# A dilated convolution with gates on one core: warm-up on zeros, a tail with early row transposes and split stores, and a new order for the scheduler

## The chip, the core and the metric

The kernel runs on one core of a Trainium2 chip. The metric is the device time of one execution in microseconds (us), lower is better. The engines of the core are TensorE (PE, with its weight loads as PEld), VectorE (DVE), ScalarE (ACT), GpSimd (POOL) and SyncE (SP), which here only issues DMAs.

## The reference

```python
B, T, D, K = (2, 16000, 144, 15)      # x: (B, T, D), w: (K, D, 2D), w_o: (D, D), all bf16
pad = (K - 1) * 2                      # dilation 2
xp = jnp.pad(x, ((0, 0), (pad, 0), (0, 0)))
h = jnp.einsum('btc,cd->btd', xp[:, pad:pad + T, :], w[0])
for i in range(1, K):
    off = pad - i * 2
    h = h + jnp.einsum('btc,cd->btd', xp[:, off:off + T, :], w[i])
f = h[..., :D]
g = h[..., D:]
return (jnp.tanh(f) * jax.nn.sigmoid(g)) @ w_o
```

A causal convolution over time with 15 taps, two steps apart, takes 144 channels to 288; the halves go through tanh and sigmoid, are multiplied, and a 144 x 144 matrix makes the output.

## The kernel before

**Tiling.** The 32,000 time steps lie as 128 partitions by 250 steps: each partition holds one stretch of time. The steps of all partitions are worked through in "octs" of eight steps, 31 in all. One matmul has 128 of the channels of one step (for 128 partitions) as stationary tile and 288 weight columns as moving data, so its output is one step of 128 stretches. The 16 channels left over are gathered eight steps at a time into tiles of 128 (XB), whose matmuls use the weights WB.

**Fewer matmuls by differences.** Taps and steps are combined as in a fast FIR filter: DVE forms differences of input tiles (V, DU, DD, BD between octs, `ef`, `diff`, `vdiff`, L731; GX, GU, GV, GD between pairs of octs, L805 to L817) and, once at the start, sums of weights (WC, WS, WD, WT, WV, L666). The products are put together again in PSUM: ACT copies partial sums from bank to bank (`copy`, L967) or into SBUF (UC, UD, XS, through `evict`, L475 and L478), POOL adds two of these into UX (L1004), DVE makes UE (written as Xp in the profile, L994) and adds UE and UX to the banks (L1068). Nearly all matmuls are issued from L823.

**Units.** Octs 1 to 30 go in 15 pairs, each pair in two units (even and odd steps), 30 units in all; oct 0 and the end of the oct ahead of it are computed more directly in a prologue. A unit u consists of blocks of matmuls, and the next unit's blocks stand between them: for unit u EF (on GV, L823; the DVE adds L1068 follow it) and DD (on GD and BD, with the weights WA and WB), for unit u + 1 CV, CD, XC, XR, SR and UP, which prepare the common sums. PJ is one third of an oct's projection. A gate on ACT and DVE (`halves`, L475/L478; `gate`, L848) makes Z; a DMA transposes Z into ZT (`ship`, L908); `project` multiplies ZT by w_o (L925), ACT casts into OS (L929), and a DMA stores an oct (L935).

**Loads.** x comes in chunks Xr of 16 steps (L517). ACT or DVE copies it compactly into STA (L691, L694), a DMA transposes STA into XA (L696). For the 16 channels left over DVE copies them into C (L682), a DMA transposes C into T (L718), and DMAs on SP bring T by way of DRAM (s) and the previous XB into XB (all at L708). All those DMAs, the transposes of Z and the stores share SP's queue and run in its order.

**What sets the order.** The code adds operations to a graph, with their dependences and a guessed duration. `schedule` and `run` simulate the engines with these guesses and fix the order of each engine's instructions before anything is built. PE takes ready operations in program order, looking at most PE_WIN operations ahead; the other engines take the one that is due first. A load that is chained by `first` gets a guessed end. ORDER holds two strings, for even and odd units, that give the program order of the blocks above. Banks of PSUM are handed out in the same simulation. So durations in the code move instructions, but have no other effect.

**Start and tail.** While the first loads are under way, PE runs 28 matmuls that nobody reads, with the identity ID and the tile ONES, both made by POOL (`warm`, L590); then it transposes the first steps of x (L618), which ACT and DVE evict into XA (L624), and DVE writes zeros into the padding (L632). The last unit's four gates don't go to Z but into rows ZL (in the profile Xr). `project_some` (L947) projects the even steps of octs 29 and 30 from ZT; `ship_pair` transposes the rows of ZL on PE (L880), copies them (L871) and projects them (L885), and `cast` (L871) brings the result to OS. The two octs are stored at L899, each in one DMA. After its last store SP waits for the semaphores of all DMAs in turn; then the program ends.

## Time and profile before

| what | value |
|---|---|
| three runs | 309.06, 309.23, 310.7 us, median 309.23 us |
| profiled execution, its own time | 308.58 us |
| its span, from first to last instruction | 306.85 us (the page rounds it to 306.9) |
| PE, DVE, ACT, POOL busy | 98%, 94%, 84%, 33% of the span |
| mean granted TensorE clock | 0.999 |
| DMA | 48.48 MB, 158 GB/s on average |

The profile describes one execution, the profiled one. Its page gives busy time, the chain of work that ended last, and the costliest groups of instructions; the views of the trace give single instructions with start and duration, and behind an arrow what ended the idle time ahead of them. A row with a count (x28) covers consecutive instructions of one kind from the start of the first to the end of the last. L823 is line 823 of the kernel before. In the kernel after the change the lines of the same operations are 4 to 11 higher: L666 becomes L670, L682 L686, L731 L735, L823 L827, L994 L1003, L1068 L1077, L925 L933, L947 L956, L885 L893, L880 L883.

### The profile page before, as it was taken

To read this page: it belongs to the slowest core of one execution; us is meant where nothing else is said; L and a number is where in the kernel's file an instruction comes from. 1 tells how busy PE (TensorE), PEld (TensorE's weight loads), DVE (VectorE), ACT (ScalarE), POOL (GpSimd) and SP (SyncE) were. 2 spreads that over 40 slices of the span, in tenths; PEclk is the share of its full clock that TensorE was granted. 3 is DMA by queue.
4 is the path that set the end of the run, shared out by engine and by line. 5 is a ranking of instruction groups with operands and counts; after the bars stand their busy time and mean duration, and the time that the engine had idled before them with its cause. 6 is when DMAs were issued, how large, how long until landed. Compare 5 with 4: busy or idle time off the path is not lost.

```text
span 306.9 us, 7442 instructions
## 1 busy us (share of the span) xinstructions
PE 299.9 (98%) x2547; PEld 235.7 (77%) x2547; DVE 289.7 (94%) x652; ACT 257.2 (84%) x812; POOL 99.8 (33%) x89
## 2 busy tenths in 40 slices
PE   7999999999999999999999999999999999999995
PEld 6777676778787787788787787777778777877784
DVE  2899999999999999999999999999999999999764
ACT  4476788988888998888898888899888889988884
POOL 7560342223333213333311333321233332123330
PEclk9999999999999999999999999999999999999999
DMA  7976647567596774759555595866647772562342
GB/s 203 310 135 152 149 138 171 118 185 179 168 169 210 121 195 127 179 168 191 180 129 139 175 179 173 159 189 146 184 134 183 191 168 62 139 132 64 93 119 115
DMA packets 100241, 48.48 MB, mean 158 GB/s; under 512 B 88269, under 2 KB 90893, under 8 KB 100203
## 3 DMA queue, kind: packets, MB, share of 16 engines
q1 hardware_dynamic: 99657, 47.62, 62.9%
q0 software_dynamic: 512, 0.33, 0.5%
q8 instruction: 20, 0.33, 0.5%
q14 instruction: 18, 0.15, 0.2%
q10 hardware_dynamic: 34, 0.05, 0.1%
HBM read 13.77 MB, written 10.20 MB: 78 GB/s over the span
## 4 chain that ended last, share of the span: by engine, by line
PE 90%; ACT 3%; DMA 2%; SPq 2%; DVE 2%; issue 1%
PE PS L823 80%; PE PS L925 9%; ACT TG L475 1%; DMA WA<-in_w_dram 1%; SPq L517 1%; DMA XB<-XB 1%; ACT PS L967 1%; DVE OS L871 1%; SPq L696 0%; SPq L528 0%; DVE Xr L871 0%; DVE WC L666 0%; ACT TG L478 0%; PE PS L654 0%; ACT UD L478 0%
## 5 line engine op out<-in xcount | busy, mean ns | idle before, releaser
L1004 POOL TENSOR_TENSOR UX<-UC,XS 128x576 f32<-128x576 f32 x60 | 84.0, 1421 | 192.8 <-ACT UC L475 134.7
L823 PE MATMUL PS<-WA,GD 128*128 128x288 bf16 x450 | 87.4, 286 | 0.0
L967 ACT ACTIVATE PS<-PS 128x288 f32<-128x288 f32 x213 | 81.3, 437 | 0.4 <-PE PS L823 0.2
L823 PE MATMUL PS<-WB,BD 128*128 128x288 bf16 x240 | 67.5, 286 | 0.0
L475 ACT ACTIVATE TG<-PS 128x288 bf16<-128x288 f32 x140 | 51.0, 432 | 14.4 <-PE PS L823 14.3
L929 ACT ACTIVATE OS<-PS 128x432 bf16<-128x432 f32 (+1 forms) x88 | 42.5, 503 | 14.7 <-PE PS L925 14.5
L823 PEld LDWEIGHTS PS<-WA,GD 128*128 128x128 bf16 x450 | 42.5, 98 | 12.9 <-DVE PS L1068 1.5
L478 ACT ACTIVATE TG<-PS 128x144 bf16<-128x144 f32 x220 | 46.0, 310 | 6.1 <-PE PS L823 6.1
L1068 DVE TENSOR_TENSOR PS<-PS,Xp 128x288 f32<-128x288 f32 x120 | 49.5, 457 | 0.9 <-PE PS L823 0.4
L1068 DVE TENSOR_TENSOR PS<-PS,UX 128x288 f32<-128x288 f32 x120 | 49.2, 455 | 0.1
L994 DVE TENSOR_TENSOR Xp<-PS,UD 128x576 f32<-128x576 f32 x60 | 43.2, 750 | 3.1 <-ACT UD L475 1.6
L823 PE MATMUL PS<-WS,GU 128*128 128x288 bf16 x210 | 44.8, 286 | 0.3 <-DMA XB<-XB 0.2
L925 PE MATMUL PS<-WOR,ZT 128*128 128x144 bf16 (+1 forms) x322 | 40.7, 253 | 0.0
L823 PE MATMUL PS<-WB,XB 128*128 128x288 bf16 x140 | 37.6, 286 | 0.0
L823 PE MATMUL PS<-WC,GV 128*128 128x288 bf16 x210 | 35.8, 287 | 0.4 <-ACT PS L967 0.4
L925 PEld LDWEIGHTS PS<-WOR,ZT 128*128 128x128 bf16 x322 | 27.8, 98 | 5.4
L823 PE MATMUL PS<-WD,DD 128*128 128x288 bf16 x210 | 31.2, 286 | 0.0
L848 DVE TENSOR_TENSOR Z<-TG 128x576 bf16<-128x576 bf16 (+1 forms) x63 | 27.5, 438 | 2.4 <-ACT TG L475 2.0
L823 PEld LDWEIGHTS PS<-WB,BD 128*128 128x128 bf16 x240 | 23.5, 98 | 5.9
L823 PEld LDWEIGHTS PS<-WS,GU 128*128 128x128 bf16 x210 | 19.8, 98 | 6.3 <-ACT PS L967 1.4
L823 PEld LDWEIGHTS PS<-WD,DD 128*128 128x128 bf16 x210 | 19.8, 98 | 6.2 <-ACT PS L967 0.9
L823 PE MATMUL PS<-WT,DU 128*128 128x288 bf16 x120 | 24.5, 286 | 0.0
(93 smaller groups left out, 469.2 us busy)
## 6 DMA issues: line engine op xcount, KB each, us to landing
out_dram<-OS SPq DMA_DIRECT2D x31, 288.0 KB, 2.5
Xr<-in_x_dram SPq DMA_DIRECT2D x15, 576.0 KB, 4.5
XB<-XB SPq DMA_DIRECT2D x30, 192.0 KB, 3.2
XB<-s SPq DMA_DIRECT2D x59, 32.0 KB, 1.9
s<-T SPq DMA_DIRECT2D x30, 32.0 KB, 3.4
WA<-in_w_dram SPq DMA_DIRECT2D x2, 288.0 KB, 4.2
ZT<-Z SPq DMA_TRANSPOSE x32, 3.1
Xp<-in_x_dram SPq DMA_DIRECT2D x2, 252.0 KB, 4.0
```

What stands on the lines that cost most here:

```text
L475: return e.activation(bass.AP(t[:].tensor, off + (0 if st > 0 else n), [[row, NP], [st, 2], [1, n]]), bass.AP(PS[:].tensor, lo * 512 + c0, ...
L478: ins = e.activation(bass.AP(t[:].tensor, off + i * n, [[row, NP], [1, n]]), bass.AP(PS[:].tensor, q.phys * 512 + c0, [[8 * 512, NP], [1, ...
L517: return e.dma_start(tile_ap, src)
L823: return lambda t: t.matmul(bank(b), lhsT=lhs(), rhs=rhs(), start=start, stop=True, skip_group_check=True)
L848: g.add("dve", lambda v: v.tensor_tensor(dst(), TG[:, s, 1, 2 * k:2 * k + n, :], TG[:, s, 0, 2 * k:2 * k + n, :], ALU.mult), r=[("TG", s, ...
L871: return (lambda e: e.activation(dst(), src(), ACT.Copy)) if eng == "act" else (lambda e: e.tensor_copy(dst(), src()))
L925: return t.matmul(PS[:, c0:c0 + n * D], lhsT=ZT[:, zt, blk_, :], rhs=WOR[:, wi_:wi_ + n, :].rearrange("p a b -> p (a b)"), start=first, st ...
L929: g.add("act", lambda e: e.activation(OS[:, os_, a:c, :].rearrange("p e d -> p (e d)"), PS[:, bo.phys * 512:bo.phys * 512 + (c - a) * D], ...
L967: g.add("act", lambda e: e.activation(bank(c), bank(b), ACT.Copy), r=[("bank", b)], w=[("bank", c)], dur=0.29, prio=prio)
L994: return v.tensor_tensor(ue(u % NU, q, 0, 2).rearrange("p (v n) -> p v n", v=2), src, UD[:, u % NUD, :, :], ALU.add)
L1004: op = g.add("pool", lambda p: p.tensor_tensor(UX[:, u % NU, h, :, :], UC[:, 0, :, :], bass.AP(XS[:].tensor, h * N2, [[2 * N2, NP], [0, 2] ...
L1068: g.add("dve", lambda e, dst=dst, src=src, ua=ua: e.tensor_tensor(bank(dst), bank(src), ua(), ALU.add), r=[("bank", src), ("UX", us, h) if ...
```

## The change

Five edits go together.

1. PE_WIN goes from 50 to 42, and both strings of ORDER are rewritten.
2. The guessed end of the loads chained by `first` comes 0.8 us earlier (`quick`); this acts on the order only.
3. The warm-up multiplies a tile HEAT of zeros by itself, which DVE clears as its first instruction, and has 34 matmuls instead of 28.
4. In the tail each gate of the last unit is followed at once by `ship_rows`: three PE transposes and a DVE copy of the rows, now in program order and not "floating" (floating operations are taken only when nothing else is ready). `ship_pair` keeps only the matmuls and the cast. `project_some` is cut two and two steps instead of three and one. Casts of oct 29 go to ACT, those of oct 30's rows to DVE, and the last third of oct 28's projection is cast on DVE instead of ACT.
5. Oct 30 is stored in two DMAs of four steps (144 KB) each instead of one of eight (288 KB).

```diff
-PE_WIN = 50
-ORDER = ("EF0 PJ EF1 XC1 CV CD0 XC0 CD1 XR0 DD00 SR0 XR1 PJ DD11 UP0 DD01 PJ UP1 SR1 DD10", "EF0 PJ EF1 DD00 XC1 CV CD0 DD01 CD1 XC0 DD10 XR1 UP0 SR0 DD11 PJ XR0 UP1 SR1 PJ")
+PE_WIN = 42
+ORDER = ("EF0 PJ EF1 XC1 CV CD0 DD00 DD01 DD10 CD1 XR1 XC0 DD11 UP0 XR0 SR0 PJ PJ SR1 UP1", "EF0 PJ EF1 XC1 CV CD0 CD1 XC0 DD00 SR0 XR0 SR1 XR1 UP0 UP1 DD01 DD10 DD11 PJ PJ")
...
-                op.end = dma_free + DMA_LAT
+                op.end = dma_free + DMA_LAT - op.quick
...
+        g.add("dve", lambda v: v.memset(HEAT[:], 0.0), w=["HEAT"], dur=0.1)
...
+            op.quick = 0.8
...
-            g.add("pe", [lambda t: t.matmul(PS[:, BANK_O * 512:BANK_O * 512 + 128], lhsT=ID[:], rhs=ONES[:], start=True, stop=True)] * n,
-                  r=["ID", "ONES"], w=[("bank", HB[BANK_O])], dur=0.07 * n)
-
-        warm(26)
+            g.add("pe", [lambda t: t.matmul(PS[:, BANK_O * 512:BANK_O * 512 + 128], lhsT=HEAT[:], rhs=HEAT[:], start=True, stop=True)] * n,
+                  r=["HEAT"], w=[("bank", HB[BANK_O])], dur=0.07 * n)
+
+        warm(32)
...
-        def ship_pair(o, h, dl, eng):
+        def ship_rows(h, dl):
+
+            q = 2 * h + (dl == 3)
+            pa = _Bank()
             c0 = h * 672 + (dl - 3) // 2 * D
             g.add("pe", [lambda t, i=i: t.transpose(PSb[:, pa.phys * 1024 + 128 * i:pa.phys * 1024 + 128 * i + 128], ZL[:, c0 + 128 * i:c0 + 128 * i + 128], ID[:]) for i in range(3)],
-                  r=[("ZL", h, 3), ("ZL", h, 7), "ID"] if dl == 3 else [("ZL", h, 7), "ID"], w=[("bank", pa)], dur=0.2, floating=True)
-            old = set(g.readers[("Xr", 0)])
-            a = g.add(eng, cast(eng, lambda: ZTL[:, q, 0:384], lambda: PSb[:, pa.phys * 1024:pa.phys * 1024 + 384]), r=[("bank", pa)], w=[("ZTL", q)], dur=0.4)
-            a.deps |= old
+                  r=[("ZL", h, 3), ("ZL", h, 7), "ID"] if dl == 3 else [("ZL", h, 7), "ID"], w=[("bank", pa)], dur=0.2)
+            a = g.add("dve", lambda e: e.tensor_copy(ZTL[:, q, 0:384], PSb[:, pa.phys * 1024:pa.phys * 1024 + 384]), r=[("bank", pa)], w=[("ZTL", q)], dur=0.27)
+            a.deps |= set(g.readers[("Xr", 0)])
...
-            g.add("act", lambda e: e.activation(OS[:, os_, a:c, :].rearrange("p e d -> p (e d)"), PS[:, bo.phys * 512:bo.phys * 512 + (c - a) * D], ACT.Copy),
+            eng = "dve" if (o, gi) == (2 * NPAIR - 2, 2) else "act"
+            g.add(eng, cast(eng, lambda: OS[:, os_, a:c, :].rearrange("p e d -> p (e d)"), lambda: PS[:, bo.phys * 512:bo.phys * 512 + (c - a) * D]),
...
-            for h, part in enumerate((dls[:3], dls[3:])):
+            for h, part in enumerate((dls[:2], dls[2:])):
...
+            ship_rows(h, 7 if k == 0 else 3)
...
-        project_some(o0, (0, 2, 4, 6), "dve")
-        ship_pair(o0, 0, 7, "dve")
-        ship_pair(o0, 0, 3, "dve")
-        store_some(o0, [0, 3, 7], 1, 8, 0)
+        project_some(o0, (0, 2, 4, 6), "act")
+        ship_pair(o0, 0, 7, "act")
+        ship_pair(o0, 0, 3, "act")
+        store_some(o0, [3, 7], 1, 8, 0)
+        ship_pair(o1, 1, 7, "dve")
+        ship_pair(o1, 1, 3, "dve")
         project_some(o1, (0, 2, 4, 6), "act")
-        ship_pair(o1, 1, 7, "act")
-        ship_pair(o1, 1, 3, "dve")
-        store_some(o1, [0, 3, 7], 1, 8, 0)
+        store_some(o1, [7], 1, 4, 4)
+        store_some(o1, [3], 1, 4, 0)
```

What the edits do to the order is read from the instructions of each engine. The first place is DVE at about 14 us of the profile, in the prologue: C is the compact copy of the 16 channels, WD and WT are sums of weights, and d_xr0 is the semaphore of the first chunk of x. Before:

```order
L731 TENSOR_TENSOR DU<-XA 128x512
L682 COPY C<-Xr 128x256 [waits d_xr0]
L731 TENSOR_TENSOR DU<-XA 128x512
L731 TENSOR_TENSOR DD<-V 128x1024 x2
L666 TENSOR_TENSOR WD<-WA 128x576 x2
L682 COPY C<-Xr 128x256 [waits d_xr1]
L666 TENSOR_TENSOR WT<-WS 128x2x288 [waits s_dve]
```

and after:

```order
L735 TENSOR_TENSOR DU<-XA 128x512 x2
L735 TENSOR_TENSOR DD<-V 128x1024
L686 COPY C<-Xr 128x256 [waits d_xr0]
L735 TENSOR_TENSOR DD<-V 128x1024
L670 TENSOR_TENSOR WD<-WA 128x576 x2
L670 TENSOR_TENSOR WT<-WS 128x2x288 [waits s_dve]
L686 COPY C<-Xr 128x256 [waits d_xr1]
```

The first copy into C has moved behind one more DU and one DD, the second behind a WT.

The second place is at about 32 us, at the end of the prologue. On PE the groups on WS,GU and WB,XB belong to XR of the first unit, those on WC,GV to its EF; d_xb9, d_xb0 and d_xb1 are semaphores of loads of XB. Before:

```order
L823 MATMUL PS<-WS,GU 128x288 [waits d_xb9,d_xb0,d_xb1]
L823 MATMUL PS<-WS,GU 128x288
L823 MATMUL PS<-WB,XB 128x288
L823 MATMUL PS<-WS,GU 128x288 x2
L823 MATMUL PS<-WB,XB 128x288
L823 MATMUL PS<-WC,GV 128x288 [waits s_dve,s_act]
L823 MATMUL PS<-WC,GV 128x288 x2
L823 MATMUL PS<-WA,GV 128x288
```

and after:

```order
L827 MATMUL PS<-WC,GV 128x288 [waits s_dve,s_act]
L827 MATMUL PS<-WC,GV 128x288 x2
L827 MATMUL PS<-WA,GV 128x288
L827 MATMUL PS<-WS,GU 128x288 [waits d_xb9,d_xb0,d_xb1]
L827 MATMUL PS<-WS,GU 128x288
L827 MATMUL PS<-WB,XB 128x288
L827 MATMUL PS<-WS,GU 128x288 x2
L827 MATMUL PS<-WB,XB 128x288
```

The group of four on GV has moved ahead of the group that waits for XB. On DVE at the same place stand the UE (Xp) sums and the adds to the banks. Before:

```order
L731 TENSOR_TENSOR V<-XA 128x1024
L994 TENSOR_TENSOR Xp<-PS,UD 128x576 [waits s_pe]
L731 TENSOR_TENSOR BD<-XB 128x1024 [waits d_xb9,d_xb0,d_xb1]
L994 TENSOR_TENSOR Xp<-PS,UD 128x576 [waits s_pe,s_dve]
L1068 TENSOR_TENSOR PS<-PS,Xp 128x288 [waits s_pe,s_act]
L1068 TENSOR_TENSOR PS<-PS,Xp 128x288 [waits s_pe]
L1068 TENSOR_TENSOR PS<-PS,Xp 128x288 [waits s_dve,s_pe]
L1068 TENSOR_TENSOR PS<-PS,Xp 128x288 [waits s_act,s_pe]
L1068 TENSOR_TENSOR PS<-PS,UX 128x288 [waits s_dve,s_pool]
L1068 TENSOR_TENSOR PS<-PS,UX 128x288 [waits s_dve]
L731 TENSOR_TENSOR DD<-V 128x1024
```

and after:

```order
L1003 TENSOR_TENSOR Xp<-PS,UD 128x576 [waits s_pe]
L735 TENSOR_TENSOR BD<-XB 128x1024 [waits d_xb9,d_xb0,d_xb1]
L1077 TENSOR_TENSOR PS<-PS,Xp 128x288 [waits s_pe,s_dve]
L1003 TENSOR_TENSOR Xp<-PS,UD 128x576 [waits s_pe]
L735 TENSOR_TENSOR V<-XA 128x1024
L1077 TENSOR_TENSOR PS<-PS,Xp 128x288 [waits s_dve]
L1077 TENSOR_TENSOR PS<-PS,Xp 128x288 [waits s_pe,s_act]
L1077 TENSOR_TENSOR PS<-PS,Xp 128x288 [waits s_act]
L735 TENSOR_TENSOR DD<-V 128x1024 [waits s_dve]
L1077 TENSOR_TENSOR PS<-PS,UX 128x288 [waits s_pool]
L1077 TENSOR_TENSOR PS<-PS,UX 128x288 [waits s_dve]
```

V has moved from ahead of the UE sums to between the adds, and DD ahead of the adds of UX.

The third place is PE's end. L925 and L947 (after: L933 and L956) project from ZT, L880 (L883) transposes the rows, L885 (L893) projects them. Before, from the last matmul of the convolution on:

```order
L823 MATMUL PS<-WB,BD 128x288
L925 MATMUL PS<-WOR,ZT 128x144 [waits s_act]
L925 MATMUL PS<-WOR,ZT 128x288
L925 MATMUL PS<-WOR,ZT 128x144
L947 MATMUL PS<-WOR,ZT 128x144 [waits d_zt0]
L947 MATMUL PS<-WOR,ZT 128x144 x7
L947 MATMUL PS<-WOR,ZT 128x144 [waits s_act,d_zt1]
L947 MATMUL PS<-WOR,ZT 128x144 x7
L880 MATMUL PS<-ID,Xr 128x128 [waits s_dve]
```

and after, from the third last matmul of the convolution on:

```order
L827 MATMUL PS<-WA,GD 128x288 x2
L827 MATMUL PS<-WB,BD 128x288
L883 MATMUL PS<-ID,Xr 128x128 [waits s_dve]
L883 MATMUL PS<-ID,Xr 128x128 x2
L933 MATMUL PS<-WOR,ZT 128x144
L933 MATMUL PS<-WOR,ZT 128x288
L933 MATMUL PS<-WOR,ZT 128x144
L956 MATMUL PS<-WOR,ZT 128x144 [waits d_zt0,s_dve]
L956 MATMUL PS<-WOR,ZT 128x144 x3
L883 MATMUL PS<-ID,Xr 128x128 [waits s_dve]
L883 MATMUL PS<-ID,Xr 128x128 x2
L956 MATMUL PS<-WOR,ZT 128x144 [waits s_dve]
```

The transposes of the rows now stand between the last matmuls and the projections; before, all twelve followed the projections from ZT.

24 lines of the change are left out of this document (13 added, 11 removed).

## The prediction

> **What bounds the kernel now.** I read the page first: the span, the busy shares and the chain that ended last.
>
> ```profile
> span 306.9 us, 7442 instructions
> PE 299.9 (98%) x2547; PEld 235.7 (77%) x2547; DVE 289.7 (94%) x652; ACT 257.2 (84%) x812; POOL 99.8 (33%) x89
> PE 90%; ACT 3%; DMA 2%; SPq 2%; DVE 2%; issue 1%
> ```
>
> TensorE (PE) is busy 98% of the span and carries 90% of the chain, VectorE (DVE) is not far behind. So only two kinds of time can go: holes in PE's stream, and the head and tail of the span. The table of windows says where the holes are; its columns are the sum, then busy time and instructions of PE, weight loads, DVE, ACT and POOL, the clock, the DMA share and GB/s.
>
> ```profile
> 14.00:32.00 18.00, 17.55 (x153) 13.65 (x150) 17.25 (x40) 13.32 (x31) 6.66 (x13) 1.00 0.68 150
> 32.00:62.00 30.00, 29.29 (x236) 21.02 (x236) 29.60 (x64) 25.05 (x83) 10.33 (x7) 1.00 0.61 147
> 62.00:80.00 18.00, 18.00 (x155) 14.41 (x153) 17.95 (x40) 15.91 (x50) 5.64 (x5) 1.00 0.67 174
> 260.00:278.00 18.00, 18.00 (x156) 14.36 (x154) 17.86 (x41) 15.84 (x51) 5.79 (x5) 1.00 0.55 116
> ```
>
> From 62 us on PE has no hole that a row shows: it is full from 62 to 80 and still full from 260 to 278. Between 14 and 62 us it is idle for 0.45 + 0.71 = 1.16 us. A hole costs more than its row shows. Here are two neighbouring rows of the timeline (start, duration, engine), a long run of matmuls, and a row of the chain:
>
> ```profile
> 31.83 0.29 PE L823 MATMUL PS<-WB,XB 128*128 128x288 bf16 x1
> 32.30 0.30 PE L823 MATMUL PS<-WS,GU 128*128 128x288 bf16 x1 [0.19 <-DMA XB<-XB]
> 10.66 3.60 PE L823 MATMUL PS<-WA,XA 128*128 128x288 bf16 x28 [0.29 <-DVE XA L632]
> 22.79 1.40 PE PS L823 x10
> ```
>
> The 28 matmuls of the third row take (3.60 − 0.16) / 28 = 0.123 us each, with 0.16 us for the drain of the last one, since a single one reads 0.29. Start to start the first two rows are 0.47 apart, so 0.35 is lost where the row says 0.19. About ten such places, the first at 22.79 and the last at 52.31 (below), make 1.16 + 10 × 0.16 = 2.8 us. This is the only stretch where a new order can win much.
>
> **The change, part by part.** All is worked out against the profiled execution: span 306.85 plus 1.73 around it, 308.58 us, which is 0.65 below the median 309.23 of the three runs.
>
> *Warm-up.* The rows of the first 11 us:
>
> ```profile
> 0.90 0.09 DVE L523 MEMSET SCR<- 128x32 uint32 x1 [0.90 <-PEq L1364]
> 1.34 0.29 POOL L569 TENSOR_SCALAR_AFFINE_SELECT ID<-ONES 128x128 bf16<-128x128 bf16 x1
> 1.68 3.17 PE L590 MATMUL PS<-ONES,ID 128*128 128x128 bf16 x28 [1.68 <-POOL XS L571]
> 4.64 1.40 PE L618 MATMUL PS<-ID,Xp 128*128 128x128 bf16 x14
> 6.32 2.38 PE L823 MATMUL PS<-WA,XA 128*128 128x288 bf16 x18 [0.28 <-DVE XA L632]
> 8.54 0.61 PE L618 MATMUL PS<-ID,Xp 128*128 128x128 bf16 x8
> 9.76 0.45 PEld L618 LDWEIGHTS PS<-ID,Xp 128*128 128x128 bf16 x8 [0.18 <-DMA Xp<-in_x_dram]
> ```
>
> Before, PE waits for POOL's ID and starts at 1.68; 28 matmuls to 4.64 are 0.106 us each. The eight transposes at 8.54 take (0.61 − 0.16) / 8 = 0.056, so the clock came up in between, during the 14 transposes. Afterwards PE waits only for the memset of HEAT, first on DVE at 0.90: at the 0.09 of SCR's row, or twice that, with the 0.05 between ID's end (1.63) and PE's start, it starts at 1.04 to 1.13. The 34 matmuls take 34 × 0.106 = 3.60, and end between 4.64 and 4.73: the transposes start 0 to 0.09 us later. The holes at 6.32 and 10.66 (DVE's memset behind its weight sums) and the wait at 9.76 for a load of x swallow that, because none of the three waits for PE. Value 0, bounds −0.1 to +0.1. A clock that comes earlier gains nothing either, as the load that lands for 9.76 comes no sooner.
>
> The Trainium skill, "TensorE: Matmul & The Clock Gate", Part 1, says that the clock is freed by about one busy, free-running window of 3.4 us, whatever the number of matmuls; the rows, 1.68 to somewhere within 4.64–6.04, agree. By it the 34 matmuls are just long enough, as an estimate, to free the clock by 4.5 us, and the 14 transposes would end 0.7 us sooner, in front of the same hidden wait. Part 4 of that page says that transposes don't count as busy for this gate; here the clock came while they ran, which leaves open whether they counted.
>
> *The start, 14 to 62 us.* The new order puts the first copy into C behind one more DU and one DD on DVE, and the first groups on WC,GV ahead of the first group on WS,GU on PE. The rows of before, DVE and then the DMA queue (SPq):
>
> ```profile
> 14.70 0.25 DVE L682 COPY C<-Xr 128x256 bf16<-128x256 bf16 x1
> 14.84 0.41 DVE L731 TENSOR_TENSOR DU<-XA 128x512 bf16<-128x512 bf16 x1
> 15.17 1.28 DVE L731 TENSOR_TENSOR DD<-V 128x1024 bf16<-128x1024 bf16 x2
> 14.98 1.21 SPq L718 DMA_TRANSPOSE T<-C  x1
> 25.74 1.84 SPq L718 DMA_TRANSPOSE T<-C  x1
> ```
>
> A DU costs 0.33 (14.84 to 15.17) and a DD half of 1.28 less the overlap, 0.60. So the copy moves from 14.70 to 15.63 and the transpose T<-C behind it from 14.98 to about 15.9. Everything queued on SP behind it (transposes of STA, s<-T, XB<-XB, XB<-s) may slide by 0.93, and the last of these is what PE waits for at 32.30. The third T<-C, at 25.74, takes 1.84 where the first took 1.21: 0.63 is waiting inside the queue, which a slide can eat. So XB lands 0.3 to 0.93 later. Against that PE has the group of four matmuls on GV, 4 × 0.123 = 0.49, ahead of that wait. Full slide: 0.93 − 0.49 = 0.44 more wait; partial slide: 0.30 − 0.49 = −0.19, of the 0.35 that is there.
>
> The next rows decide how that reaches the adds in PSUM, for which the groups on WA,GD wait:
>
> ```profile
> 31.20 0.69 DVE L731 TENSOR_TENSOR V<-XA 128x1024 bf16<-128x1024 bf16 x1
> 32.15 0.76 DVE L994 TENSOR_TENSOR Xp<-PS,UD 128x576 f32<-128x576 f32 x1 [0.27 <-PE PS L823]
> 34.35 1.56 DVE L1068 TENSOR_TENSOR PS<-PS,Xp 128x288 f32<-128x288 f32 x4 [0.17 <-ACT XS L475]
> 52.31 0.54 PE L823 MATMUL PS<-WC,GV 128*128 128x288 bf16 x3 [0.37 <-ACT PS L967]
> ```
>
> The changed order puts a V (0.60) and a DD (0.60) between the adds of the first unit. Behind the V the second add ends 0.6 later if nothing slid, 1.0 with the slide; PE has two other groups, 0.5, to cover it. What DVE did early it needn't do later: the V and DD are gone from the following unit, so up to 0.7 comes back before 45 us. At 52.31 PE waits 0.37 for a PSUM copy on ACT; in the new order one group of three matmuls (0.37) less stands ahead of it, of which the copy's own lead covers about half: +0.2. I take +0.25 for the stretch. The ends are −0.5, when the slide vanishes and the 0.35 at 32.30 goes, and +1.0, when both the slide and the inserted V reach PE with nothing given back.
>
> *The steady part, 62 to 297 us.* Each pair of units issues the same instructions as before; only their order differs, and PE_WIN lets PE look less far ahead. DVE has 17.95 of 18 us taken from 62 to 80. Two rows of the view of waits, DVE from 62 to 296 us (total, times, longest):
>
> ```profile
> DVE Xp L994 <- ACT UD L475: 1.6, 1, 1.6
> DVE Z L848 <- ACT TG L475: 1.4, 1, 1.4
> ```
>
> These waits of DVE, 3.0 us, left PE full, so buffers absorb a slip of 1.5 us. PE can gain nothing here and can lose only where a buffer is short. I take +0.1, bounds −0.3 (small stalls that go) to +0.5 (a wait like the one at 32.30, 0.35, once, with its consequences).
>
> *The tail.* The rows of before:
>
> ```profile
> 300.17 1.16 PE L947 MATMUL PS<-WOR,ZT 128*128 128x144 bf16 x16
> 301.17 1.01 PE L880 MATMUL PS<-ID,Xr 128*128 128x128 bf16 x12
> 302.11 1.18 PE L885 MATMUL PS<-WOR,Xr 128*128 128x144 bf16 x12
> 300.75 0.82 DVE OS L871 x2
> 301.49 0.30 DVE L848 TENSOR_TENSOR Xr<-TG 128x288 bf16<-128x288 bf16 x1
> 301.70 0.88 DVE L871 COPY Xr<-PS 128x384 bf16<-128x384 bf16 x3
> 302.57 1.22 DVE L871 CAST OS<-PS 128x288 bf16<-128x288 f32 x3
> 303.42 0.81 SPq L899 DMA_DIRECT2D out_dram<-OS  x2
> out_dram<-OS SPq DMA_DIRECT2D x31, 288.0 KB, 2.5
> ```
>
> Before, all transposes wait until 301.17, then three row copies (about 0.26 each in starts) and three casts (0.41 each) go through DVE in series, and the second of the two last stores is issued near 303.42 + 0.43 = 303.85; 2.5 later, at 306.3, it lands, and the span ends at 306.85. Afterwards six of the twelve transposes stand at the last convolution matmuls and six among the projections. PE's work up to the end is the same, 303.29 before; it saves the hole between 301.17 + 12 × 0.056 = 301.84 and 302.11, 0.27, and ends at 303.0. The last gate is on DVE at about 301.1 instead of 301.49, since the two casts at 300.75 (0.82), which stood in front of it, go to ACT, and a copy of rows comes in their place. After it come three transposes, a row copy on DVE (301.8 to 302.15), three matmuls and a cast (to 303.26); ACT casts the last four columns of steps behind PE's end, 303.06 to 303.47 by the 0.41 of such a cast. So the last issue moves from 303.85 to about 303.65, and a store of half the bytes lands at least 0.2 sooner than 2.5. That gives an end at 306.35: −0.5. Bounds −0.2, if a half store lands no faster, and −0.7, if it takes half the time beyond the issue's 0.4.
>
> The Trainium skill, "DMA: Bandwidth & Descriptors", "Latency and other measured facts", puts a fixed cost of about 2 us on a DMA, most of it the receipt's round trip; this speaks against the halved store. The row's 2.5 us for 288 KB fits it, and by it the half store would give −0.3 instead of −0.5, as an estimate.
>
> **Sum.** 0 + 0.25 + 0.1 − 0.5 = −0.15: 308.43 for an execution like the profiled one, 309.1 with the 0.65 to the median. The bounds add up to −1.6 at best (−0.1 − 0.5 − 0.3 − 0.7) and +1.4 at worst (0.1 + 1.0 + 0.5 − 0.2), so 307.6 to 310.6 around 309.23.
>
> **The rivals.**
>
> *The start's holes close.* DVE now does V and DD before they are needed and PE takes ready groups ahead of the XB wait; if that halves the 2.8 us lost between 14 and 62, it is −1.4 there, and with −0.5 in the tail the time is 309.23 − 1.9 = 307.3. For it: every hole there is a short wait for a neighbour's work, which order alone can cover. Against it: DVE's first C copy, at the head of the queue that XB waits for, is later by 0.93.
>
> *VectorE slips.* DVE is taken for 17.95 of 18 us. If the new order costs each of the 14 pairs of units one short wait that it doesn't have now, 0.25 us like the 0.27 at 32.15, DVE falls behind PE by 14 × 0.25 = 3.5 us and PE waits for the adds: 309.23 + 3.5 − 0.5 = 312.2. It decides from the point where DVE's total slip passes the 1.5 us that the buffers took above. Against it: the waits of 1.6 and 1.4 us left no mark on PE.
>
> *Zeros don't free the clock.* If operands of zero don't count as work, the gate opens only on the transposes from 4.70, about 3.9 us later (before: 1.68 to some 5.5), at 8.6. The 18 matmuls of 6.32 then cost 0.123 more each, 2.2, of which the holes at 9.76 and 10.66 hide about 0.45: 309.23 + 1.8 − 0.15 = 310.9. Nothing in the trace of before shows zeros; that 28 matmuls on a constant pattern counted speaks mildly against it.
>
> *The warm-up brings nothing* because the load at 9.76 hides it: this is in the forecast.
>
> **How the numbers follow.** Forecast, 307.6 to 310.6 with 309.1 as its centre: 0.60. Start's holes close, 307.3: 0.20. VectorE slips, 312.2: 0.11. Zeros stay cold, 310.9: 0.07. Something else: 0.02, slower as likely as faster. The range goes from 306.9, below the second case, to 311.2, above the fourth; it leaves out VectorE's slip and little else. What a measurement of this kernel can tell from no change is about 0.5%, 1.55 us: 307.68 and 310.78 are the edges. Faster is the second case and the forecast's lowest edge: 0.22. Slower is the third, and most of the fourth case: 0.18. Same: 0.60.
>
> **What would show it.** Warm-up: PE's first matmul near 1.1 us, transposes at 4.7, and the first groups of 288 columns at 0.123 each; if 18 of them take 4.4 us, the zeros stayed cold. Start: T<-C near 15.9 on the queue, PE idle in the windows 14–32 and 32–62 adding up to 1.0 to 1.6 where it was 1.16; below 0.6 the second case holds. Steady part: PE 18.00 of 18 in each window; any window below 17.9 speaks for VectorE's slip, with the adds of PSUM named as its releaser. Tail: from the last convolution matmul to the end of the span 0.5 less than before, with the last half store issued 0.2 sooner. The prediction is wrong if the middle of the kernel changes by more than 0.5 us, since I found no work there that is added or taken away.

## The result, and the profile after

The change made the kernel slower: 311.24 us (median of 8 runs, 310.92 to 312.93) against 309.14 us for the kernel before (8 runs, 308.64 to 310.7) on the same chip. The ratio is 1.0076, with a 95% interval of 1.0057 to 1.0096 (the quotient of the two medians is 1.0068). The forecast was 309.1, no difference. The profiled execution of the changed kernel took 310.92 us, with a span of 309.19, which is 2.34 longer than the 306.85 of before. The page of the changed kernel, with the chain's shares in the last row:

```profile
span 309.2 us, 7467 instructions
PE 300.3 (97%) x2553; PEld 235.3 (76%) x2553; DVE 289.7 (94%) x652; ACT 258.3 (84%) x812; POOL 101.3 (33%) x89
PE 85%; DVE 6%; SPq 3%; DMA 2%; issue 1%; ACT 1%
```

PE's busy time has risen by only 0.4, so 1.9 of the 2.34 are idle time of PE. In the chain PE gives 5 points away, and DVE gains 4. The windows of the changed kernel, in the columns known from the prediction:

```profile
14.00:32.00 18.00, 17.55 (x154) 13.79 (x152) 16.82 (x40) 12.89 (x30) 6.79 (x14) 1.00 0.66 134
32.00:62.00 30.00, 27.84 (x222) 19.76 (x220) 28.59 (x63) 23.28 (x74) 10.29 (x6) 1.00 0.65 152
62.00:80.00 18.00, 18.00 (x154) 14.17 (x152) 17.89 (x40) 15.87 (x49) 5.54 (x4) 1.00 0.60 156
140.00:180.00 40.00, 39.87 (x336) 31.01 (x334) 39.36 (x87) 35.85 (x123) 11.09 (x8) 1.00 0.65 162
260.00:278.00 18.00, 18.00 (x154) 13.87 (x152) 17.91 (x40) 15.83 (x51) 5.55 (x4) 1.00 0.54 121
```

From 32 to 62 us PE is idle for 2.16, where it was 0.71. After that only the window from 140 to 180 shows a hole, 0.13.

**How I add it up.** I give each matmul a position: its start minus the time that all matmuls ahead of it need at the rate of the long runs (0.1226 us for 288 columns, which the rows round to 0.123; others in proportion), the warm-up left out. The position only grows where PE loses time, so the same amount of finished work (P, in us of matmul time) can be compared between two traces whatever the order. The numbers are worked out from the single rows of both traces.

| at P | about, us | before | after | difference | what lies ahead of it |
|---|---|---|---|---|---|
| 16 | 22 | 6.06 | 6.46 | +0.40 | prologue |
| 24 | 31 | 6.86 | 7.26 | +0.40 | |
| 26 | 34 | 7.28 | 8.18 | +0.90 | wait for XB |
| 28 | 37 | 7.47 | 9.08 | +1.61 | adds of the first unit |
| 38 | 48 | 8.13 | 10.07 | +1.94 | second unit |
| 60 | 71 | 9.08 | 11.07 | +1.99 | |
| 291 | 303 | 10.39 | 12.82 | +2.43 | middle |
| span's end | 309 | | | +2.34 | tail |

So the prologue has +0.40, the start +1.59, the middle +0.44 and the tail −0.09. The prologue's part is chance: the value at P 16 lies between 6.00 and 6.89 over the twenty profiled executions of this study, and from 6.06 to 6.74 among those whose prologue is that of before; I take it to be the landing of the first loads, which I did not follow. The start is the loss, and not by an accident of this one pair of executions. From P 24 to P 60 the six profiled executions with the start's order of before (before, e4, e12, e16, e17, e18, all told of below) lose 2.2 to 3.5 us, with a median of 2.5; the three with the start's order of the change (the change, e8, e15) lose 3.8, 4.0 and 5.0, and e1 4.1.

**Warm-up.** PE's first rows in the changed kernel:

```profile
1.07 3.44 PE L594 MATMUL PS<-HEAT 128*128 128x128 bf16 x34 [1.07 <-DVE SCR L526]
4.35 0.72 PE L622 MATMUL PS<-ID,Xp 128*128 128x128 bf16 x10
9.84 0.61 PE L622 MATMUL PS<-ID,Xp 128*128 128x128 bf16 x8 [0.56 <-DMA Xp<-in_x_dram]
```

The ten transposes take (0.72 − 0.16) / 10 = 0.056 each from 4.35 on, the full rate. So the zeros freed the clock, and they did so before the transposes: the record of the granted clock has it at 3.98. When it comes differs between executions: from 3.84 to 7.11 us in the twelve with zeros, from 4.36 to 7.64 in the eight with the identity. The time won ends in the wait of 0.56 for x, as forecast.

**Start.** DVE's copy into C, then the rows of SP's queue in the changed kernel:

```profile
16.01 0.21 DVE L686 COPY C<-Xr 128x256 bf16<-128x256 bf16 x1
```

```profile
16.25 1.22 SPq L722 DMA_TRANSPOSE T<-C  x1
...
26.89 1.79 SPq L722 DMA_TRANSPOSE T<-C  x1
...
31.44 0.58 SPq L712 DMA_DIRECT2D XB<-s  x1
```

Less the 0.40 of the prologue the copy stands at 15.61 and T<-C at 15.85, as forecast (15.63 and 15.9). The third T<-C went from 25.74 to 26.89, and still takes 1.79: in this pair its waiting inside the queue did not eat the slide. Over more executions it ate some of it: the third T<-C takes 1.84 to 2.80, 2.33 on average, in the six with the start's order of before, of which the profiled execution of before is the shortest, and 1.76 to 2.17, 1.96 on average, in six with late copies (the change, e1, e6, e8, e11, e15). The chain of the changed kernel (start, time, what; "issue" is time in which the engine waits for nothing that the profile shows) tells how this goes on:

```profile
31.44 2.65 DMA XB<-s
34.08 0.05 issue
34.13 0.56 PE PS L827 x3
34.71 0.46 DVE PS L1077
35.17 0.66 DVE Xp L1003
35.83 0.07 DVE V L735
35.90 0.45 issue
36.34 0.47 DVE PS L1077
36.81 0.05 issue
36.86 1.31 PE PS L827 x9
```

XB lands at 34.09, and the chain leaves PE for DVE: an add, the second UE sum (Xp), V, and again an add, in series, before PE can go on at 36.86. PE's waits from 14 to 62 us (total, times, longest), where before only two waits for ACT, 0.8 in all, and one of 0.2 for XB stood:

```profile
PE PS L827 <- ACT PS L976: 1.3, 3, 0.7
PE PS L827 <- DVE PS L1077: 0.5, 2, 0.2
PE PS L827 <- DMA XB<-s: 0.4, 1, 0.4
PE PS L933 <- issue: 0.3, 1, 0.3
```

**Tail.** ACT, DVE, SP and PE in the changed kernel, then the stores of its last microseconds (count, size, median time from issue to landing):

```profile
303.39 2.53 ACT L876 ACTIVATE OS<-PS 128x288 bf16<-128x288 f32 x6
304.76 0.95 DVE L876 CAST OS<-PS 128x288 bf16<-128x288 f32 x2
304.95 1.63 SPq L907 DMA_DIRECT2D out_dram<-OS  x3
305.06 0.41 PE L956 MATMUL PS<-WOR,ZT 128*128 128x144 bf16 x4
```

```profile
out_dram<-OS SPq DMA_DIRECT2D x2, 288.0 KB, 2.1
out_dram<-OS SPq DMA_DIRECT2D x2, 144.0 KB, 1.8
```

The three last stores are issued in a row, one at 304.95, two from 305.74 on, and the last issue ends at 304.95 + 1.63 = 306.58. The span ends 2.61 later. Before, it ended 2.63 after the last issue (303.42 + 0.81 = 304.23, rounded up by 0.01; the end 306.85), with a whole store, 2.45 from issue to landing, as the last one. The half store landed at 308.01, 1.43 after the end of its issue, but the end did not follow it.

### The profile page after: what moved, and what is told of

It is laid out like the page before. It is cut to its first block, busy times and chain, and to the rows that moved or that the text cites. A ratio compares the mean times of both kernels' runs of the same rounds, so it can differ in the third digit from the quotient of the medians.

```text
span 309.2 us, 7467 instructions
## 1 busy us (share of the span) xinstructions
PE 300.3 (97%) x2553; PEld 235.3 (76%) x2553; DVE 289.7 (94%) x652; ACT 258.3 (84%) x812; POOL 101.3 (33%) x89
## 4 chain that ended last, share of the span: by engine, by line
PE 85%; DVE 6%; SPq 3%; DMA 2%; issue 1%; ACT 1%
PE PS L827 75%; PE PS L933 9%; DMA WA<-in_w_dram 1%; DMA XB<-s 1%; DVE V L735 1%; SPq L519 1%; SPq L712 1%; DVE PS L1077 1%; DVE DD L735 1%; SPq L722 1%; DVE DU L735 1%; ACT PS L976 0%; SPq L700 0%; DVE WC L670 0%; DVE WT L670 0%
## 5 line engine op out<-in xcount | busy, mean ns | idle before, releaser
L1013 POOL TENSOR_TENSOR UX<-UC,XS 128x576 f32<-128x576 f32 x60 | 85.2, 1441 | 194.2 <-ACT UC L477 141.7
L976 ACT ACTIVATE PS<-PS 128x288 f32<-128x288 f32 x213 | 83.0, 439 | 0.6 <-PE PS L827 0.2
L477 ACT ACTIVATE TG<-PS 128x288 bf16<-128x288 f32 x148 | 52.8, 425 | 14.1 <-PE PS L827 13.9
L480 ACT ACTIVATE TG<-PS 128x144 bf16<-128x144 f32 x204 | 43.7, 312 | 5.9 <-PE PS L827 5.5
L933 PE MATMUL PS<-WOR,ZT 128*128 128x144 bf16 (+1 forms) x322 | 38.5, 253 | 0.3 <-issue 0.3
L933 PEld LDWEIGHTS PS<-WOR,ZT 128*128 128x128 bf16 x322 | 27.2, 98 | 5.6 <-ACT XS L477 0.6
```

The costliest lines, as they stand in the source:

```text
L477: return e.activation(bass.AP(t[:].tensor, off + (0 if st > 0 else n), [[row, NP], [st, 2], [1, n]]), bass.AP(PS[:].tensor, lo * 512 + c0, ...
L480: ins = e.activation(bass.AP(t[:].tensor, off + i * n, [[row, NP], [1, n]]), bass.AP(PS[:].tensor, q.phys * 512 + c0, [[8 * 512, NP], [1, ...
L933: return t.matmul(PS[:, c0:c0 + n * D], lhsT=ZT[:, zt, blk_, :], rhs=WOR[:, wi_:wi_ + n, :].rearrange("p a b -> p (a b)"), start=first, st ...
L976: g.add("act", lambda e: e.activation(bank(c), bank(b), ACT.Copy), r=[("bank", b)], w=[("bank", c)], dur=0.29, prio=prio)
L1013: op = g.add("pool", lambda p: p.tensor_tensor(UX[:, u % NU, h, :, :], UC[:, 0, :, :], bass.AP(XS[:].tensor, h * N2, [[2 * N2, NP], [0, 2] ...
```

## The experiments

All times are medians beside runs of the kernel before on the same chip; ratios have a 95% interval and need not be the quotient of the two medians. "P" and positions are those of the table above, each from one profiled execution.

### Which edit costs the time

**e1: Edit 2 alone, in the kernel before.**

```diff
+            op.quick = 0.8
```

> The kernel before with edit 2 alone (the guessed end of the first loads 0.8 us earlier). The order of its instructions at 14 us and at 32 us is that of the changed kernel: the first copy into C behind two DU and one DD, V and DD between the adds. Theory A (these guesses make the loss of the start, by the late copy into C and the late adds): the first T<-C on the queue near 15.9 instead of 14.98, XB for the first unit 0.9 to 1.3 us later, and a time 1.5 to 2.0 us above the kernel before, so about 310.6 to 311.2. Theory B (the new strings and PE_WIN make it): within 0.5 us of the kernel before.

318.47 against 309.4: ratio 1.0302 (1.0269 to 1.0336). The position at P 26, 28 and 60 is 8.07, 8.97 and 10.96, as in the changed kernel (8.18, 9.08, 11.07), although the two strings are the old ones. **The guessed ends make the loss of the start.** In the middle the old strings lose 9.0 with these guesses, where before lost 1.3: the position goes from 10.96 at P 60 to 19.97 at P 291, with rows such as this one, and a window of the clock (1.00 is full speed) behind it:

```profile
239.50 0.42 PE L825 MATMUL PS<-WA,GD 128*128 128x288 bf16 x2 [2.25 <-DVE GD L814]
```

```profile
240.70:244.10 3.40, 3.40 (x17) 2.13 (x16) 3.25 (x7) 2.78 (x13) 0.00 (x0) 0.50 0.78 215
```

**e2: The change without edit 2.**

```diff
-            op.quick = 0.8
+            op.quick = 0.0
```

> The changed kernel without edit 2 (new strings, PE_WIN, zeros and tail stay). Theory A: the start is that of the kernel before, PE idle 14 to 62 us about 1.2 instead of 2.6; what stays is up to +0.45 of the middle and -0.1 of the tail, so 0 to +0.5 us against the kernel before, 309.1 to 309.7. Theory B: it stays as slow as the changed kernel, about 311.

313.12: ratio 1.0125 (1.01 to 1.015). The start is that of before: 9.63 at P 60, of which 0.41 is the prologue, so 0.14 is lost. But the middle loses 6.3 (before 1.3), up to 15.90 at P 291. The new strings with the old guesses are worse than both kernels, as the old strings with the new guesses were: strings and guesses belong together.

**e3: Edit 1 alone, in the kernel before.**

```diff
-PE_WIN = 50
+PE_WIN = 42
```

and the two new strings of ORDER.

> The kernel before with edit 1 alone (the strings and PE_WIN). Theory A: within 0.5 us of the kernel before, at most +0.45 from the middle. Theory B: 1.5 to 2.1 us slower.

313.42: ratio 1.013 (1.0103 to 1.0157). The profiled execution took longer than that (316.15), with one long wait for XB. PE's row, and the window behind it:

```profile
34.92 0.55 PE L823 MATMUL PS<-WS,GU 128*128 128x288 bf16 x2 [1.93 <-DMA XB<-s]
```

```profile
35.10:38.50 3.40, 3.40 (x17) 2.25 (x16) 2.20 (x5) 1.06 (x2) 1.30 (x1) 0.50 0.68 146
```

Here too the middle loses, 5.0. The median tells the same as the run before: without the new guesses the new strings cost about 4 us.

**e4: Edits 4 and 5 alone (the tail), in the kernel before.**

```diff
+            ship_rows(h, 7 if k == 0 else 3)
...
+        store_some(o1, [7], 1, 4, 4)
+        store_some(o1, [3], 1, 4, 0)
```

with the casts and the cut of `project_some` of the change.

> The kernel before with edits 4 and 5 alone (rows transposed behind each gate, oct 30 in two stores). Theory T (after the last store is issued, SP's row of waits for the semaphores takes a fixed 2.6 us, which the earlier landing doesn't shorten): last issue ends 0.1 us earlier, time 0 to -0.1 us, end of the span 2.6 us behind the end of the last issue in both kernels. Rival (the landing of the last store ends the span, as I forecast): -0.5 us. If the tail's new order itself costs something, it is slower.

311.0: ratio 1.0055 (1.0035 to 1.0074). I had looked for a gain. From the last matmuls of the convolution to the end of the span it is 0.06 shorter than before, about what the whole change gives (0.09). The loss lies earlier: the position goes from 10.93 at P 240 to 13.03 at P 270, where before it went from 10.15 to 10.39. The windows row of this run:

```profile
260.00:278.00 18.00, 17.27 (x140) 12.10 (x138) 17.87 (x40) 14.96 (x53) 6.07 (x4) 1.00 0.44 107
```

PE is idle for 0.73 in a stretch that the diff does not touch. The scheduler keeps the best of ten passes for the whole graph, and with another tail it settles on another order 25 to 45 us ahead of it.

**e12: Edit 3 alone (zeros), in the kernel before.**

```diff
-                  r=["ID", "ONES"], w=[("bank", HB[BANK_O])], dur=0.07 * n)
+                  r=["HEAT"], w=[("bank", HB[BANK_O])], dur=0.07 * n)
...
-        warm(26)
+        warm(32)
```

> The kernel before with edit 3 alone: 34 warm-up matmuls on zeros, from 1.07 us. By the changed kernel's trace the zeros free the clock before 5 us, and the load of x and DVE's weight sums hide what that gains: within 0.3 us of the kernel before. If the earlier warm-up did something to the loads, the eight transposes behind the fourth piece of x start later than 9.8 us and it is 0.3 to 0.5 us slower.

309.36 against 309.35: ratio 1.0009 (0.9982 to 1.0036). No difference, as forecast.

### What happens in the start

**e5: The change with the two copies into C moved early again, on DVE alone.**

```diff
+        dq = g.order["dve"]
+        for cp, n in ((copies[0], 2), (copies[1], 1)):
+            i = dq.index(cp)
+            dq.insert(i - n, dq.pop(i))
```

> The changed kernel with one difference: on DVE the two first copies into C stand where they stood before (behind one DU; behind the two WD). Theory S (the slide of the DMA queue makes the loss of the start): the queue's first T<-C 0.9 us earlier than in the changed kernel, XB for the first unit 0.9 earlier, PE's 0.57 us wait for it near 34 us goes and part of the 0.9 us for the adds behind it: 0.9 to 1.5 us faster than the changed kernel, so 309.8 to 310.4. Theory V (V and DD between the adds make it): at most 0.5 us faster, from the wait for XB alone.

311.13 (12 runs): ratio 1.0045 (1.0024 to 1.0066). The position at P 28 falls from 9.08 to 8.17, 0.17 of it by the prologue, so 0.74 is won by then; at P 38 it is 10.06, the 10.07 of the change. All of it is lost again between 42 and 47 us. Rows of DVE and POOL of this run:

```profile
42.04 0.68 DVE L737 TENSOR_TENSOR DD<-V 128x1024 bf16<-128x1024 bf16 x1
42.64 1.89 DVE L737 TENSOR_TENSOR BD<-XB 128x1024 bf16<-128x1024 bf16 x1
```

```profile
42.12 3.67 POOL L1015 TENSOR_TENSOR UX<-UC,XS 128x576 f32<-128x576 f32 x2 [3.53 <-ACT UC L477]
```

The same BD takes 1.89 instead of 0.68, while POOL adds UX. The Trainium skill, "SBUF — State Buffer", "SBUF: two separate sides", says that DVE and GpSimd share a pair of SBUF ports under an exclusive lock, and that an operation of DVE with two SBUF inputs and one of GpSimd that reads SBUF exclude each other for a whole instruction. The single rows agree, one standing still for the other: DD ends at 42.72, the first UX at 43.98, BD at 44.53 and the second UX at 45.80. The distances, 1.26, 0.55 and 1.27, are a little under what the three take alone (1.41, 0.68, 1.41), although in its row each begins while the one ahead still runs.

**e6: The change with V ahead of the first UE sum, and DD behind the first adds of UX.**

```diff
+        dd = dq.pop(i + 5)
+        dq.insert(i + 7, dd)
+        dq.insert(dq.index(sums[0]), dq.pop(i + 1))
```

> The changed kernel with V moved ahead of the first UE sum on DVE and the DD behind the first adds of UX, as before; the copies into C stay late. Theory V: PE's waits for the adds at 36 to 37 us (0.88) go, 0.9 to 1.5 us faster than the changed kernel. Theory S: at most 0.5 us faster, because XB still lands late and V now stands ahead of a sum that is ready.

311.99: ratio 1.0074 (1.0048 to 1.01). Nothing is won; here too the BD takes 1.90 (at 43.62).

**e7: Both moves together.**

> The changed kernel with both moves of DVE's order undone (copies into C, V and DD). If the two are the whole loss of the start, 1.4 to 1.8 us faster than the changed kernel: 309.5 to 309.9, with PE's idle time of 14 to 62 us near 1.2 us. If it is something else that the guesses changed, it stays above 310.5.

311.66: ratio 1.0071 (1.0044 to 1.0099). The position is 8.27 at P 28, 0.8 better than in the change, and 10.44 at P 38, 0.4 worse. The BD at 43.01 takes 1.90. So the two moves do close most of the first loss, and a collision takes their gain.

**e9: The early copies and the third BD ahead of GV.**

```diff
+        i = dq.index(sums[2]) - 1
+        dq.insert(i - 2, dq.pop(i))
```

> The changed kernel with the first two copies into C early, as in the run that moved them alone, and the third BD on DVE ahead of GV instead of behind DD. In that run PE gained 0.85 us by 35 us and lost it again near 46 us: BD took 1.89 us instead of 0.68, begun while POOL's UX ran (POOL's two UX spanned 3.67 us instead of 2.77), and the adds behind it came late. Theory P (DVE and POOL shut each other out, and the collision took the gain): BD takes 0.68 us here, and the kernel is 0.9 to 1.3 us faster than the changed one: 310.0 to 310.4. Rival (DVE is simply full, so that what is gained at one place is lost at the next): within 0.4 us of the changed kernel.

311.11: ratio 1.0062 (1.0041 to 1.0083). This missed: the BD takes 0.68, but now the DD in its place takes 1.88 (43.20 to 45.08). A move on DVE only changes who collides.

**e13: Both moves, and POOL's first UX of the second unit waits for that BD.** This takes away the collision itself.

```diff
+        ups[1, 0].deps.add(dq[dq.index(sums[2]) - 1])
```

> The changed kernel with copies into C, V and DD moved back on DVE as in an earlier run, and POOL's first UX of the second unit waiting for the BD on DVE. Without that wait UX started at 42.62 and BD took 1.90 us (0.68 elsewhere), and all that was gained by 35 us was lost by 48. Theory P (the collision of DVE and POOL at this place takes it back): BD takes 0.68 us, PE is 1.0 to 1.2 us further at 50 us than in the run without the wait, and the time is 310.3 to 310.7. Rival (DVE is full anyway, or PE waits for something else there): within 0.4 us of the run without the wait, 311.3 to 312.

310.69 (12 runs): ratio 1.0031 (1.0009 to 1.0052), and 0.97 less than the run with both moves alone. DVE and POOL of this run:

```profile
42.43 0.68 DVE L737 TENSOR_TENSOR BD<-XB 128x1024 bf16<-128x1024 bf16 x1
43.05 0.76 DVE L1006 TENSOR_TENSOR Xp<-PS,UD 128x576 f32<-128x576 f32 x1
```

```profile
43.19 2.78 POOL L1017 TENSOR_TENSOR UX<-UC,XS 128x576 f32<-128x576 f32 x2 [5.40 <-ACT PS L978]
```

BD is back at 0.68, POOL's pair is down from 3.67 to 2.78, and the position at P 38 is 8.97, 1.47 better than with the moves alone. Of that 0.19 lies in the prologue and 0.51 between it and P 36, ahead of the collision; from P 36 to P 38 the moves alone lose 1.20 and this run 0.43. These 0.77 the collision is shown to carry. DVE's Xp sum, which has only one input in SBUF, runs beside POOL in its usual 0.76. In the profiled execution of the change itself DVE won and POOL waited:

```profile
43.54 0.68 DVE L735 TENSOR_TENSOR BD<-XB 128x1024 bf16<-128x1024 bf16 x1
```

```profile
43.02 3.83 POOL L1013 TENSOR_TENSOR UX<-UC,XS 128x576 f32<-128x576 f32 x2 [3.53 <-ACT UC L477]
```

So there it cost less, 0.43 from P 36 to P 38 (before 0.19); in the profiled execution of the run with one store, below, the same order had a BD of 1.89 and lost 1.32. The collision is not new with the change. In the kernel before, too, POOL waited at this place (the pair alone takes 2.78):

```profile
41.50 3.63 POOL L1004 TENSOR_TENSOR UX<-UC,XS 128x576 f32<-128x576 f32 x2 [4.33 <-ACT UC L475]
```

The code's simulation keeps such operations of DVE and POOL apart (`lock`), but by its guessed times, which are not those of the trace.

**e11: The kernel before with the copies late, as in the change.**

```diff
+            dq.insert(i + n, dq.pop(i))
```

> The kernel before with one difference: on DVE the first copy into C stands behind one more DU and a DD, the second behind a WT, as in the changed kernel. Theory S (the late copy slides the queue, and PE waits for XB): XB for the first unit 0.9 us later, PE's wait near 32 us longer by 0.5 to 0.9, and 0.4 to 1.0 us slower than the kernel before at 62 us, 309.6 to 310.3. Rival (the slide is absorbed, the loss comes only with V and DD between the adds): within 0.3 us of the kernel before.

310.45 (12 runs): ratio 1.0045 (1.0026 to 1.0064), 1.1 us for two copies of 0.2 us that stand a little later. PE's row:

```profile
34.63 0.42 PE L825 MATMUL PS<-WS,GU 128*128 128x288 bf16 x2 [1.37 <-DMA XB<-s]
```

The slide arrives at the wait for XB, and none of it comes back: the position is 10.99 at P 60 against 9.08, of which 0.42 is the prologue. The other 1.49, all lost by P 26, are more than the slide of 0.93, as this wait differs between executions by itself: from P 24 to P 26 the profiled execution of before loses 0.42, that of e17, with the same order there, 1.67.

### What happens in the tail

**e15: The change with one store for oct 30, as before.**

```diff
-        store_some(o1, [7], 1, 4, 4)
-        store_some(o1, [3], 1, 4, 0)
+        store_some(o1, [3, 7], 1, 8, 0)
```

> The changed kernel without edit 5: oct 30 in one store of 288 KB. PE and DVE run in the same order. Theory T (SP's waits end the span 2.6 us behind the end of the last issue): the one store is issued about when the second half was, the span behind the last matmul is the same within 0.1 us, so the time is that of the changed kernel. Rival (the half store's earlier landing counts): 0.4 to 0.5 us slower.

312.02 (7 runs): ratio 1.0074 (1.0046 to 1.0102), no different from the change as far as its time goes. Its trace tells more. SP's row:

```profile
306.13 1.33 SPq L907 DMA_DIRECT2D out_dram<-OS  x2
```

The last issue ends at 307.46, and the position at P 291 is 14.00, so 293.46 us lie between; in the change it is 306.58 − 12.82 = 293.76, before 304.22 − 10.39 = 293.83. The new tail by itself wins 0.37, and the second half store costs 0.30 of that. The span ends 2.61 after the last issue, as with the half stores.

**Why 2.61?** After its last store SP waits for 58 semaphores. The trace has 29 single rows for it, about 0.061 us apart, with one pause of 0.36 to 0.38 that no semaphore explains: 29 × 0.061 + 0.37 = 2.14, and 0.47 for the end of the program. All fifteen traces with the waits at the end, with half or whole stores, end 2.61 to 2.63 after their last issue. The next runs put nearly all of these waits ahead of the fourth last store (third last in the kernel before), where SP is idle anyway:

```diff
+                if name == "sp" and i == len(plan[name]) - 4:
+                    for s, v in g.finals:
+                        if (s, v) not in st_last:
+                            eng.wait_ge(s, v)
```

In the change:

> The changed kernel with the final waits of SP for all semaphores but those of the last four stores put ahead of the fourth last store, where SP is idle; two instructions with the four waits for the stores are left behind the last one. Theory T (the row of 29 waits, 2.6 us, ends the span, and hides the earlier landing of the half store at 1.9 instead of 2.45 us): the span ends about 0.6 us behind the landing of the last store, 0.5 to 0.7 us faster than the changed kernel. Rival (the landing ends the span): within 0.1 us of the changed kernel.

In the early copies with BD ahead:

> The same, with the final waits of SP put ahead of the fourth last store. From the span of the run with the early waits alone (0.29 us less behind the last matmul than in the changed kernel) 0.3 us less than the run beside it: 309.7 to 310.1 if theory P holds.

In the version in which UX waits for BD:

> The same with SP's final waits ahead of the fourth last store: 0.3 us less than the run beside it, 310.0 to 310.4 by theory P.

In the kernel before:

> The kernel before with SP's final waits ahead of its third last store. Before, the last store landed at 306.30 and the wait for it stood at 306.37 in the row: the landing now ends the span, 0 to 0.1 us less than before, which the runs can't tell from no change.

| run | median, us | ratio (95%) | ratio of the kernel that it was made from | end after the last issue, us |
|---|---|---|---|---|
| e8_waits_early | 311.61 | 1.0065 (1.0038 to 1.0093) | 1.0076 | 2.25 |
| e10_copy_bd_waits | 310.83 | 1.0038 (1.001 to 1.0065) | 1.0062 | 2.25 |
| e14_ux_and_waits_early | 310.51 | 1.0029 (1.0006 to 1.0051) | 1.0031 | 2.30 |
| e16_before_waits_early | 310.23 | 1.0029 (1.0005 to 1.0054) | 1 | 2.83 |

In the first three the end now follows the landing of the last store, 0.31 to 0.36 sooner, but their medians can't tell that from nothing. In the kernel before it failed: SP's pause fell between the last two stores (305.005 to 305.373), the last one landed 2.34 after the end of its issue (before 2.08), and the median was 0.85 worse.

### Putting it together

**e17: The kernel before with edits 4 and 5, and with the order of before kept for all that stands ahead of the last gates.** A table gives each engine's order of before as soft dependences.

```diff
+        for t in PIN.values():
+            l = [self.ops[int(i)] for i in t.split()]
+            for a, b in zip(l, l[1:]):
+                b.soft.add(a)
```

> The kernel before with edits 4 and 5 (the tail, with two stores for oct 30), every instruction ahead of the last unit's gates kept in the order of the kernel before. The tail alone, without this, was 1.6 us slower, and its trace loses 2.1 us between 255 and 275 us, where the new tail had moved other instructions. Theory O (that loss is order, not tail): the loss at 255 to 275 us is gone and the time is within 0.3 us of the kernel before, the span behind the last convolution matmuls 0.1 us shorter. Rival (the tail itself costs it): 1.2 to 2 us slower again.

309.12 (12 runs) against 309.41: ratio 0.9984 (0.9954 to 1.0013). The windows row of this run, to be held against that of the tail alone:

```profile
260.00:278.00 18.00, 18.00 (x154) 14.35 (x153) 17.91 (x40) 16.01 (x51) 5.55 (x4) 1.00 0.48 118
```

PE is full again, and the 1.6 us that the tail alone lost against the kernel before are gone. The loss was the order's, not the tail's.

**e18: The same with one store and without the waits that earlier waits of SP imply** (3 of the 58 semaphores are left).

```diff
+        self.finals = [(s, v) for s, v in self.finals if known["sp"].get(s, 0) < v]
...
-        store_some(o1, [7], 1, 4, 4)
-        store_some(o1, [3], 1, 4, 0)
+        store_some(o1, [3, 7], 1, 8, 0)
```

> The kernel before, order kept as in the run beside it, with the new tail but one store for oct 30, and without those final waits of SP that its earlier waits already imply: three waits, for stores, are left of 58. Theory T: the single last store gives 0.4 us (as the changed kernel's runs with one store and with two differ by 0.30 behind the last matmul, and the tail with two is 0.09 shorter than before), the missing waits another 0.1 to 0.4, until the landing of the last store ends the span 0.5 us behind it: 0.5 to 0.8 us faster than the kernel before. Rival (the tail's gains don't show in the time): within 0.3 us.

**308.49** (12 runs, 308.11 to 309.47) against 309.41: ratio 0.9966 (0.9947 to 0.9984). This version is faster than both kernels. SP's row in its profile:

```profile
303.14 1.33 SPq L918 DMA_DIRECT2D out_dram<-OS  x2
```

The last issue ends at 304.47 and the span at 306.76, 2.29 later, 0.50 behind the landing at 306.26. From P 291 to the end it is 306.76 − 10.99 = 295.77, where before it was 306.85 − 10.39 = 296.46: 0.69 won, 0.36 by the tail up to the last issue and 0.33 by the waits. The median is 0.63 below that of the run before, which is what the 0.30 of the second store and the 0.33 of the waits add up to; but the intervals of the two ratios overlap.

## Why the prediction was wrong

1. **Warm-up, 0: right.** The zeros freed the clock, the wait for x hid it, and alone it makes no difference (ratio 1.0009). The 34 matmuls ended at 4.35, not at 4.64 to 4.73, as the clock came while they ran.
2. **Start, +0.25: this is the step that failed.** It measured +1.59, beyond its upper bound of +1.0. The slide was named rightly and to 0.05 us. What failed are the offsets that I set against it, and the giving back. The wait for XB grew by 0.50, about the full slide's 0.44 and not a value between −0.19 and 0.44: in this pair the third T<-C did not eat 0.63 of the slide ("0.63 is waiting inside the queue, which a slide can eat"), and over more executions it ate 0.4 on average. Behind the V the adds cost 0.71, where I had 0.1 to 0.5. And that "up to 0.7 comes back before 45 us" did not happen: between P 28 and P 38 another 0.33 went, 0.24 of it at the place where DVE and POOL exclude each other. That mechanism the prediction doesn't have; but it is at work in the kernel before as well, and that it makes these 0.24 is not shown. The 0.2 at 52.31 became 0.31 (P 42 to 44), against 0.25 that came back just before it (P 38 to 42). So every piece went to its bad end: the chain shows them as links, XB, PE, the adds, PE, and I had priced them as if they were independent. My bound was too low even by my own pieces, which at their worst make 0.44 + 0.5 + 0.2 = 1.14. The late copies alone cost 1.1 (e11).
3. **Middle, +0.1: inside its bounds.** It measured +0.44, most of it near 160 to 190 us (0.77 from P 135 to P 180, before 0.39). But the reasoning behind it was thin. With the same work the runs with edit 2 alone, without edit 2, with edit 1 alone and with the tail alone lost 9.0, 6.3, 5.0 and 3.3 us there (from P 60 to P 291), where before lost 1.3: that PE "can lose only where a buffer is short" did not say how often an order makes it short.
4. **Tail, −0.5: it measured −0.09.** PE's part came: 0.37 up to the end of the last issue with one store, where I had 0.2. The second half store gave 0.30 of that back, as its issue stands in the same queue; I had counted no issue for it. And that "a store of half the bytes lands at least 0.2 sooner" is right (1.43 after the end of its issue, where the one store of e15 took 1.80 and that of before 2.08) but ends nothing, because SP's row of waits lasts 2.61 whatever lands. I took the end of the span for the landing plus a constant, which it nearly was before: landing at 306.30, end at 306.85. The sum was loose as well: 0.2 and 0.2 make −0.4 and not −0.5, and half of the 2.1 beyond the issue would have put the far bound at −1.25 and not −0.7.
5. **The rivals.** None of the three describes it. The start's holes didn't close but doubled (1.16 to 2.61 of idle time). DVE did become the releaser in the start, though not in each pair of units, as that rival had it. The range ended at 311.2, just below 311.24.

The cause of the slower time is thus settled for the start: edit 2's guesses (e1, e2). They put the copies late, which alone costs 1.1 (e11), and V and DD between the adds, whose part no run shows by itself (with V and DD moved back alone, e6, nothing is won); and undoing both wins only when the collision of DVE and POOL behind them is taken away too (e13). What stays open: how much each of the two costs in the change; how the 0.44 of the middle divides between strings and window; why in one execution POOL waits and in another DVE; and what SP's pause of 0.37 us is.

## What to carry to other kernels

A small operation at the head of a queue of DMAs can cost its whole slide when it comes late: follow it along the queue to the engine that waits, and let nothing come back unless a row shows slack there. A table of orders and the guesses that it goes with are one thing: the strings alone made this kernel slower by 4.0 us, the guesses alone by 9.1, and even a new tail cost 1.6 by moving work some 40 us ahead of it; fix the order of the rest before you measure an edit of a part. At the end of a program, look at what the last engine does after its last issue: waits that earlier waits imply can hide the landing that you speed up.
